# An adaptive-norm transformer block: gates and second shift and scale as rows from column-tiled products, first chunk modulated in SBUF, and a written-out sequence

## The chip, the cores and the metric

The kernel runs on one core of a Trainium2 chip. The metric is the device time of one execution in microseconds (us); a kernel's time is the median of its runs. Engines are named as in the profile: PE (TensorE, products), PEld (its weight loads), DVE (VectorE), ACT (ScalarE), POOL (GpSimd), SP (SyncE, which here issues nearly all DMAs).

## The reference

One sequence of 2048 rows of 640 values goes through windowed attention and a gated MLP. A vector c gives shifts, scales and gates for both. All inputs are bfloat16.

```
mod = silu(c) @ w_mod                      # 640 -> 6 x 640
sa, ca, ga, sb, cb, gb = mod
h = layernorm(x) * (1 + ca) + sa
x = x + ga * (attention(h @ wqkv) @ wo)    # 32 heads of 20, causal, window 256
h = layernorm(x) * (1 + cb) + sb
x = x + gb * ((sigmoid(h @ w_gate) * (h @ w_up)) @ w_down)   # hidden size 1536
```

## The kernel before

The rows are worked in 8 chunks of 256. For each chunk: normalize (DVE, line 811; POOL for some, 808), turn so that features lie on partitions, multiply by 1 + ca and add sa (chunks 0 and 1: turned by PE, and modulated by ACT or DVE on the way out of PSUM, lines 849 and 850; later chunks: turned by a transposing DMA, line 818, and modulated in SBUF, lines 826 and 827), project to q, k and v, attend, project with wo, add to x, normalize again, turn by DMA into h2T, modulate with shB and scB, and run the MLP. Scores use a 32-row tiling of PE and one PSUM tile S of four banks, which exp (ACT, line 1005) empties; products of probabilities and V (line 706, E and V) use a 32-column tiling. All other products take a PSUM bank of the pool M, of which there are four.

The gates are folded into weights: wo is scaled by ga (line 1228) and w_down by 0.5 gb (line 1163), both through one tile gbc, which holds the gate's 640 values on all 128 partitions.

How w_mod is used. It is loaded in four parts: part 0 (first shift and scale) into the place of w_down, part 1 (ga and sb) into that of w_up, part 2 (cb) into that of hh, part 3 (gb) into that of w_down again, once part 0 is used. silubc holds silu(c) repeated along a free axis. `mod_cols` makes a shift or a scale as a column, with w_mod as the stationary operand: five 128-column blocks by five slices, 64 equal result columns each, of which one is kept. `mod_bc` makes a gate on all partitions, with silubc (128 columns) as the stationary operand and w_mod as 320 moving columns: two halves by five slices, and two scalings into gbc (line 753). `mod_bc` and `mod_cols` run once for ga and sb, and once for gb and cb. The first shift and scale are made by similar products into S, copied to mA (line 776). Ahead of these, PE runs products on zeros that only keep it busy (lines 686 and 697).

What sets the order of the work. Every instruction group is recorded with its engines, its cost and its dependencies. `schedule` then places the groups one after the other by a table of priorities (PRIO), with a planner's model of costs, latencies and DMA bandwidth. Each engine runs its own list in order; waits between engines are semaphores. DMAs are placed in the lists of SP or ACT like instructions: a DMA that waits holds up what stands behind it on that engine. Tile slots are handed out by the planner too.

Of the kernel before, what the change touches and what calls it, by code (L numbers as in the profile page):

```python
# [51 lines left out]
class Tile:  # L52
    __slots__ = ("pool", "name", "res", "slot", "ops", "left", "rel", "prev", "mate")
# [27 lines left out]
class Prog:  # L81
# [8 lines left out]
    def op(self, eng, fn, dur, reads=(), writes=(), prio=50.0, lat=0.05, work=None, tmin=0.0, extra=(), tag="", hold=(),  # L90
# [13 lines left out]
        o.prio = PRIO[self.seq] if self.seq < len(PRIO) else prio  # L104
# [46 lines left out]
    def schedule(self):  # L151
# [3 lines left out]
        cand = {e: {} for e in ENGS}  # L155
# [6 lines left out]

        def arm(o):
            t = o.tmin
            for d in o.deps:
                t = max(t, d.end + (0.0 if (d.eng == "pe" and o.engs == ("pe",)) else d.lat))
            o.ready = t
            for e in o.engs:
                cand[e][o.seq] = o

        def slot_time(pool, s):
            ten = pool.tenant[s]
            if ten is None:
                if not all(x.done for x in pool.init[s]):
                    return None
                return max([x.end + x.lat for x in pool.init[s]], default=0.0)
            if ten.left:
                return None
            return max(x.end + x.lat for x in ten.rel)

        def slots_for(o):

            st = 0.0
            taken = {}
            got = []
            for t in o.tiles:
                if t.slot is None and t.mate is not None:
                    if any(g[0] is t for g in got):
                        continue
                    bs = None  # L190
                    for s in range(0, len(t.pool.tenant), 2):
                        ra, rb = slot_time(t.pool, s), slot_time(t.pool, s + 1)
                        if ra is not None and rb is not None and (bs is None or max(ra, rb) < bs[0]):
                            bs = (max(ra, rb), s)
                    if bs is None:
                        return None
                    got += [(t, bs[1]), (t.mate, bs[1] + 1)]
                    st = max(st, bs[0])
                elif t.slot is None:
                    bs = None  # L200
                    used = taken.setdefault(t.pool, set())
                    for s in range(len(t.pool.tenant)):
                        if s in used:
                            continue
                        rt = slot_time(t.pool, s)
                        if rt is not None and (bs is None or rt < bs[0]):
                            bs = (rt, s)
                    if bs is None:
                        return None
                    used.add(bs[1])  # L210
                    got.append((t, bs[1]))
                    st = max(st, bs[0])
                else:
                    for x in t.prev:
                        st = max(st, x.end + x.lat)
            return st, got

        for o in self.ops:
            if o.nleft == 0:
                arm(o)  # L220
        n = len(self.ops)
        placed = 0
        while placed < n:
            best = None
            for e in ENGS:
                c = cand[e]
                if not c:
                    continue
                lst = []
                tmin = None  # L230
                for o in c.values():
                    st = max(free[e] + (SWITCH if e == "pe" and o.mode != pemode else 0.0), o.ready)
                    if e == "dve" and o.port:
                        st = max(st, free["pool"])
                    elif e == "pool":
                        st = max(st, portend)
                    if o.isdma:
                        st = max(st, bw - QMAX)
                    if o.tiles:
                        got = slots_for(o)  # L240
                        if got is None:
                            continue
                        st = max(st, got[0])
                    lst.append((st, o))
                    if tmin is None or st < tmin:
                        tmin = st
                if not lst:
                    continue
                eps = PE_EPS if e == "pe" else 0.04
                pick = min((x for x in lst if x[0] <= tmin + eps), key=lambda x: (x[1].prio, x[1].seq))  # L250
                if best is None or pick[0] < best[0]:
                    best = (pick[0], e, pick[1])
            if best is None:
                left = [(o.tag, o.engs, [t.pool.name for t in o.tiles if t.slot is None]) for e in ENGS
                        for o in cand[e].values()][:40]
                raise RuntimeError(f"no op can be placed: {placed} of {n}: {left}")
            st, e, o = best
            for x in o.engs:
                cand[x].pop(o.seq, None)
            o.eng = e  # L260
            for t, s in slots_for(o)[1]:
                ten = t.pool.tenant[s]
                t.prev = list(t.pool.init[s]) if ten is None else list(ten.rel)
                t.slot = s
                t.pool.tenant[s] = t
# [7 lines left out]
            if o.isdma:  # L273
                turn = o.dlat > 3.0
                bw = max(st + o.dlat, bw + (MIXED if turn != lastturn and bw > st + o.dlat else 0.0)) + o.work
# [13 lines left out]
            placed += 1  # L289
# [12 lines left out]
            for x in o.succ:  # L302
                x.nleft -= 1
                if x.nleft == 0:
                    arm(x)
# [90 lines left out]
def c_pe(n):  # L396
# [3 lines left out]
PE_EPS = 0.14  # L400
PRIO = [
# [106 lines left out]
TR1 = 2  # L508
NPH = 2
NPQ = 2  # L510
PQ = ()
KEEP = 3
DSAFE = 1.0
MIXED = 0.39
NPB = 0
OUTE = ("sp", "act")
XE = ("sp", "act")
MW = 64
AFTER = 1
NOW = 1  # L520
# [10 lines left out]
def build(nc, A_x, A_wqkv, A_wo, B_x, B_w_gate, B_w_up, B_w_down, c, w_mod, out, S=2048):  # L531
# [298 lines left out]
    def pe_transposes(src, dst, sc, sh, Rmod, prio, a, ln="a"):  # L830
        last = []
        for dt in range(NDT):
# [10 lines left out]
            if a == 0 and dt == 3 and ln == "a":  # L843
                fills.append(fill(2 * FILL, [o]))
# [440 lines left out]
```

## Time and profile before

| what | value |
|---|---|
| median of 3 runs | 337.96 us |
| lowest and highest run | 336.16 and 338.79 us |
| the profiled execution: span | 333.9 us |
| median less that span | 4.1 us |
| PE, DVE, ACT, POOL busy | 325.6, 222.4, 229.3, 180.5 us |
| granted PE clock | full from 7 us to the end |
| bytes moved by DMA | 37.73 MB, of them 20.97 MB read from HBM |

The profile is one execution. Its span runs from the first to the last instruction; a run's time holds some us more, and the profiled execution's own time outside of its span is not listed, so it is compared by its span. A busy PE need not be at its peak, since products overlap: the distance from start to start of consecutive products says what one costs. Idle time counts only on the engine that sets the end.

The DMA engines are 70% to 90% busy in the first 80 us, in which all weights are loaded, and 0% to 50% later:

```profile
DMA  7999998984653773047125501501320303102101
```

### The profile page before, as it was taken

Reading aid. Unit: us, or ns where it says so; the run is one execution under the profiler, and the core shown is the slowest. Engines: PE = TensorE matmul, PEld = TensorE weight load, DVE = VectorE, ACT = ScalarE, POOL = GpSimd, SP = SyncE. Lnnn points to the kernel's source line nnn. Section 1 sums busy time; section 2 is a strip of 40 time slices with the busy share of each in tenths; the row PEclk is TensorE's granted clock in tenths of the full one; section 3 lists DMA queues with packets and bytes.
Section 4 is the critical chain, followed back from the end, with each engine's and each line's share of the span. In section 5 each row is a group of like instructions: output and inputs, shape, how many; then the busy total and the mean of one; then the engine's idle time right before and its main releaser. Section 6 shows DMA issues by size and latency. Waiting matters only on the chain.

```text
span 333.9 us, 10066 instructions
## 1 busy us (share of the span) xinstructions
PE 325.6 (98%) x4142; PEld 232.0 (69%) x4142; DVE 222.4 (67%) x445; ACT 229.3 (69%) x218; POOL 180.5 (54%) x259
## 2 busy tenths in 40 slices
PE   7899989998999999999999999999999999999996
PEld 2667646665786667766776776776776777887885
DVE  5389987999969845874486638465856295746323
ACT  1597977878768787888689967895695869221220
POOL 5038988996468764656565656665454667001000
PEclk9999999999999999999999999999999999999999
DMA  7999998984653773047125501501320303102101
GB/s 239 380 375 313 239 261 178 289 187 74 120 97 80 120 124 89 23 101 101 66 61 105 100 26 42 117 22 43 71 67 22 104 2 77 42 24 61 41 0 39
DMA packets 72694, 37.73 MB, mean 113 GB/s; under 512 B 46538, under 2 KB 71370, under 8 KB 72650
## 3 DMA queue, kind: packets, MB, share of 16 engines
q1 hardware_dynamic: 71056, 35.31, 43.9%
q10 hardware_dynamic: 1594, 1.80, 1.7%
q8 instruction: 32, 0.52, 0.6%
q14 instruction: 12, 0.10, 0.1%
HBM read 20.97 MB, written 5.24 MB: 79 GB/s over the span
## 4 chain that ended last, share of the span: by engine, by line
PE 86%; DVE 6%; DMA 3%; issue 2%; SPq 1%; ACT 0%; DVEq 0%
PE M L705 70%; PE S L706 8%; PE M L706 6%; DMA wd<-in_w_mod_dram 3%; PE S L686 2%; SPq L603 1%; DVE st L791 1%; DMA x<-in_A_x_dram 1%; DVE Tn L1059 1%; DVE T L1052 1%; DVE On L1061 1%; DVE x L811 1%; PE S L705 1%; DVE stg L885 1%; DVE h2T L827 0%
## 5 line engine op out<-in xcount | busy, mean ns | idle before, releaser
L1005 ACT ACTIVATE E<-S 128x2048 bf16<-128x2048 f32 x90 | 169.1, 1878 | 44.5 <-PE S L706 42.7
L1013 POOL TENSOR_SCALAR_AFFINE_SELECT E<-E 128x512 bf16<-128x512 bf16 (+2 forms) x90 | 78.2, 869 | 40.2 <-ACT E L1005 40.1
L1015 POOL TENSOR_SCALAR_AFFINE_SELECT E<-E 128x512 bf16<-128x512 bf16 (+1 forms) x84 | 68.5, 815 | 47.7 <-ACT E L1005 44.4
L705 PE MATMUL M<-h2T,wg 128*128 128x256 bf16 x480 | 64.8, 273 | 1.0 <-DVE h2T L827 1.0
L705 PE MATMUL M<-h2T,wu 128*128 128x256 bf16 x480 | 65.2, 273 | 0.0
L1182 DVE SCALAR_TENSOR_TENSOR hh<-sig,M 128x512 bf16<-128x512 f32 x48 | 32.6, 681 | 44.4 <-ACT sig L1180 24.4
L705 PE MATMUL M<-wd,hh 128*128 128x320 bf16 (+2 forms) x396 | 58.4, 295 | 0.0
L705 PEld LDWEIGHTS M<-h2T,wg 128*128 128x128 bf16 x480 | 45.0, 98 | 10.6 <-issue 2.3
L705 PEld LDWEIGHTS M<-h2T,wu 128*128 128x128 bf16 x480 | 45.3, 98 | 9.4 <-issue 3.0
L1180 ACT ACTIVATE sig<-M 128x512 f32<-128x512 f32 x48 | 28.3, 596 | 29.0 <-PE M L705 29.0
L705 PEld LDWEIGHTS M<-wd,hh 128*128 128x128 bf16 x396 | 37.1, 98 | 14.5 <-issue 1.5
L706 PE MATMUL S<-QT,KT 20*128 20x256 bf16 (+1 forms) x960 | 35.9, 245 | 0.2
L1201 DVE TENSOR_TENSOR x<-M,x 128x320 bf16<-128x320 f32 (+2 forms) x33 | 15.7, 479 | 23.4 <-PE M L705 22.9
L791 DVE BATCH_NORM_STATS2 st<-x 128x6 f32<-128x320 bf16 x64 | 28.3, 475 | 3.6 <-DMA x<-in_A_x_dram 3.5
L1052 DVE STREAM_TRANSPOSE T<-M 128x512 f32<-128x512 f32 x32 | 21.3, 697 | 12.7 <-PE S L706 12.0
L706 PEld LDWEIGHTS S<-QT,KT 20*128 20x128 bf16 x960 | 14.1, 92 | 20.1 <-ACT E L1005 12.1
L705 PE MATMUL M<-wk,hT 128*128 128x320 bf16 x160 | 26.6, 300 | 0.1
L705 PE MATMUL M<-wq,hT 128*128 128x320 bf16 x160 | 25.7, 299 | 0.2 <-issue 0.2
L705 PE MATMUL M<-wv,hT 128*128 128x320 bf16 x160 | 25.3, 300 | 0.1
L705 PE MATMUL M<-wo,oT 128*128 128x320 bf16 x160 | 24.1, 300 | 0.0
L706 PEld LDWEIGHTS M<-E,V 128*32 128x32 bf16 x960 | 20.0, 97 | 4.2 <-issue 2.6
L706 PE MATMUL M<-E,V 128*32 128x256 bf16 (+1 forms) x960 | 22.8, 246 | 0.2 <-issue 0.2
(78 smaller groups left out, 316.5 us busy)
## 6 DMA issues: line engine op xcount, KB each, us to landing
x<-in_A_x_dram SPq DMA_DIRECT2D x20, 160.0 KB
doc<-On SPq DMA_DIRECT2D x64, 40.0 KB
wd<-in_w_mod_dram SPq DMA_DIRECT2D x6, 320.0 KB
wd<-in_B_w_down_dram SPq DMA_DIRECT2D x4, 480.0 KB
wu<-in_w_mod_dram SPq DMA_DIRECT2D x5, 320.0 KB
out_dram<-x SPq DMA_DIRECT2D x10, 160.0 KB
oT<-doc SPq DMA_DIRECT2D x8, 192.0 KB
wg<-in_B_w_gate_dram SPq DMA_DIRECT2D x2, 576.0 KB
```

What stands on the lines that cost most here:

```text
L603: return e.dma_start(dst(), src())
L686: ins = e.matmul(p_S.aps[0][:, 3, :], Eall[:, 0, 0:128], Eall[:, 0, 128:640], start=True, stop=True)
L705: return e.matmul(o, l, r, start=st, stop=sp, skip_group_check=True)
L706: return e.matmul(o, l, r, start=st, stop=sp, tile_position=tp, skip_group_check=True)
L791: A("dve", lambda e, g, bi=bi, j=j: e.bn_stats(v(bi * 12 + j * 6, 6), src[bi].ap[:, j * 320:(j + 1) * 320]), 0.48, reads=[src[bi].r()], wr ...
L1005: A("act", lambda e, eng: e.activation(E.ap[:], Sp.ap[:], ACT.Exp, scale=SM_SCALE), 1.876, reads=[Sp.r()], writes=[E.r()], prio=3, tag=f"e ...
L1013: return e.affine_select(ap, ap, pattern=[[0, ap.shape[1]], [1, 128]], compare_op=ALU.is_ge, fill=0.0, base=0, channel_multiplier=-1)
L1015: return e.affine_select(ap, ap, pattern=[[0, ap.shape[1]], [-1, 128]], compare_op=ALU.is_ge, fill=0.0, base=-1, channel_multiplier=1)
L1052: A("dve", lambda e, g, h=h: e.transpose(T1.ap[:, 512 * h:512 * h + 512], X[h].ap), 0.694, reads=[X[h].r()], writes=[T1.r(h)], prio=3.5, t ...
L1180: A("act", lambda e, g, pg=pg, sg=sg: e.activation(sg.ap[:], pg.ap[:], ACT.Tanh, scale=0.5), c_act(512), reads=[pg.r()], writes=[sg.r()], ...
L1182: A("dve", lambda e, g, pu=pu, sg=sg, f0=f0: e.scalar_tensor_tensor(out=hh.ap[:, f0:f0 + 2, :], in0=sg.ap[:].rearrange("p (a b) -> p a b", ...
L1201: A("dve", lambda e, g, ps=ps, bi=bi, c0=c0, n=n: e.tensor_tensor(x1[bi].ap[:, c0:c0 + n], ps.ap[:, 0:n], x1[bi].ap[:, c0:c0 + n], op=ALU. ...
```

## The change

1. Both gates, the second shift and the second scale come from one kind of product, `mod_tiles`. The stationary operand is 32 columns of silubc, in one of four column tiles; each tile takes 160 columns of w_mod, and the result is a row, 32 times over, in each of four groups of 32 partitions. One call makes a gate and a shift (or scale): 5 slices x 2 x 4 = 40 products, as one group that waits for all its slices.
2. A gate's row (`mod_gate`) is scaled into `grow`, stored to DRAM (1280 bytes) and loaded back to all partitions of gbc. A shift or scale (`mod_turn`) is turned to columns by DVE's 32x32 transpose, its blocks picked so that feature t*128+p comes to partition p.
3. silubc is 64 wide, not 128. 
4. Chunk 0: its turned x is copied out of PSUM without shift and scale, and modulated in SBUF by DVE, ACT or POOL.
5. The table of priorities goes; the place and engine of every group are written out (PLAN, one number for each: 5 times the group's number plus the engine's), and `schedule` only follows it. The order differs on all engines. Among other things c's load is the first DMA on ACT, ahead of x; on SP the first part of w_mod goes ahead of x; PE runs two products on zeros before it turns c, and twelve after it (before: eight, and six after); part 3 of w_mod is issued behind the first transpose of chunk 2; all five scalings of wo are on DVE (before: two, with three on POOL).
6. Some of the planner's costs differ (DMA work and latency); they have no effect but through PLAN's slots.

```diff
+    def mod_tiles(parts, prio):
+        ps = Tile(p_M, "modt")
+
+        def fn(e, g):
+            ins = None
+            for kt in range(NDT):
+                for n, (i, c0, turned_) in enumerate(parts):
+                    src = wm_ap[i][:, kt, c0:c0 + D]
+                    for j in range(4):
+                        if turned_:
+                            r = src.rearrange("p (t g c) -> p g t c", g=4, c=32)[:, j]
+                            o = ps.ap[32 * j:32 * j + 32, n * 160:n * 160 + 160].rearrange("p (t c) -> p t c", c=32)
+                        else:
+                            r = src[:, j * 160:j * 160 + 160]
+                            o = ps.ap[32 * j:32 * j + 32, n * 160:n * 160 + 160]
+                        ins = mm(e, o, silubc[:, kt, 0:32], r, kt == 0 and n == 0, kt == NDT - 1, tp=(0, 32 * j))
+            return ins
...
+    def mod_gate(ps, n, factor, prio):
+        g = dram(f"gate{prio}", [4, 160])
+        Rd = R("gdram")
+        A("dve", lambda e, _: e.tensor_scalar(grow[:], ps.ap[:, n * 160:n * 160 + 160], factor, None, op0=ALU.mult),
...
+        dma(lambda: g, lambda: grow[0:128:32, :], 0.05, reads=[R_grow], writes=[Rd], prio=1, tag="gout", dur=0.42)
+        dma(lambda: gbc[:], lambda: g.rearrange("(o a) b -> o (a b)", o=1).to_broadcast([128, D]), 0.45, reads=[Rd], writes=[R_gbc],
...
+    def mod_turn(dst, ps, n, prio, plus, Rdst):
+        A("dve", lambda e, _: e.transpose(mt[:], ps.ap[:, n * 160:n * 160 + 160]), c_dve(160), reads=[ps.r()], writes=[R_mt], prio=8,
...
+        A("dve", lambda e, _: e.tensor_scalar(dst[:], mt[:].rearrange("p (t c) -> p t c", c=32)[:, :, 0], plus, None, op0=ALU.add), 0.2,
...
     def pe_transposes(src, dst, sc, sh, Rmod, prio, a, ln="a"):
...
+            if a == 0:
+                evac(lambda dt=dt: dst.ap[:, dt, :], lambda ps=ps: ps.ap[:, 0:256], 256, [ps.r()], [dst.r(dt)], 1, f"{ln}hTe{a}")
+                continue
...
             turned[a] = pe_transposes(src, t, scA, shA, [R_mA], 1, a)
+            if a == 0:
+                modulate(t, scA, shA, [R_mA], 1, "a", a, src)
...
-    o1 = mod_bc(1, 0, 1.0, 18)
-    psB = Tile(p_M, "modB")
-    cB, o2 = mod_cols(1, 640, psB, 18)
...
+    psB, o1 = mod_tiles([(1, 0, False), (1, D, True)], 18)
+    mod_gate(psB, 0, 1.0, 18)
+    mod_turn(shB, psB, 1, 18, 0.0, R_shB)
...
-    o3 = mod_bc(3, 0, 0.5, 19)
-    psC = Tile(p_M, "modC")
-    cC, o4 = mod_cols(2, 0, psC, 19)
...
+    psC, o3 = mod_tiles([(3, 0, False), (2, 0, True)], 19)
+    p_hh.init[1].append(o3)
+    mod_gate(psC, 0, 0.5, 19)
+    mod_turn(scB, psC, 1, 19, 1.0, R_scB)
```

More of the change, by code (lines that the diff above doesn't have):

```diff
@@ L52 @@
 class Tile:
-    __slots__ = ("pool", "name", "res", "slot", "ops", "left", "rel", "prev", "mate")
+    __slots__ = ("pool", "name", "res", "slot", "ops", "left", "rel", "prev", "mate", "at")
     def __init__(self, pool, name):
@@ L178, in slot_time @@
                 return None
[L179 to L185, printed above, removed]
-            for t in o.tiles:
[L187 to L259, printed above, removed]
-            o.eng = e
[L261 to L265, printed above, removed]
@@ new lines, in schedule @@
+        assert sorted(x // 5 for x in PLAN) == list(range(len(self.ops)))
+        for code in PLAN:
+            o, e = self.ops[code // 5], ENGS[code % 5]
+            assert e in o.engs and all(d.done for d in o.deps), (o.tag, e)
+            st = max(free[e] + (SWITCH if e == "pe" and o.mode != pemode else 0.0), o.tmin)
+            for d in o.deps:
+                st = max(st, d.end + (0.0 if d.eng == "pe" and o.engs == ("pe",) else d.lat))
+            if e == "dve" and o.port:
+                st = max(st, free["pool"])
+            elif e == "pool":
+                st = max(st, portend)
+            if o.isdma:
+                st = max(st, bw - QMAX)
+            for t in o.tiles:
+                if t.slot is None:
+                    place(t)
+                    if t.mate is not None:
+                        st = max(st, t.mate.at)
+                st = max(st, t.at)
+            o.eng = e
```

105 lines of the change are left out of this document (45 added, 60 removed), and 215 rows, old and new, of tables (PLAN, PRIO).

## The prediction

> **What bounds the kernel now.** I read the busy shares first, then TensorE's waits, then the timeline of TensorE and the chain of waits. Busy shares and the whole list of TensorE's waits:
>
> ```profile
> PE 325.6 (98%) x4142; PEld 232.0 (69%) x4142; DVE 222.4 (67%) x445; ACT 229.3 (69%) x218; POOL 180.5 (54%) x259
> ```
> ```profile
> PE S L686 <- DVE E L681: 1.7, 1, 1.7
> PE M L705 <- DMA wd<-in_w_mod_dram: 1.3, 1, 1.3
> PE M L705 <- DVE h2T L827: 1.0, 2, 0.6
> PE M L705 <- DVE hT L850: 0.6, 1, 0.6
> PE M L705 <- DVE stg L885: 0.4, 1, 0.4
> PE M L705 <- issue: 0.2, 1, 0.2
> PE M L706 <- issue: 0.2, 1, 0.2
> ```
>
> TensorE is the bound: it waits 5.4 us in 333.9, and after 83 us never. So two things can move the end: products taken out of its stream, and the few waits before 83 us. These timeline rows (start, length, engine, line, what) price both:
>
> ```profile
> 10.75 0.38 PE L697 MATMUL S<-E 128*128 128x512 bf16 x1
> 11.76 0.28 PE L705 MATMUL M<-ident,x 128*128 128x128 bf16 x2 [0.63 <-DVE hT L850]
> 12.26 1.52 PE L705 MATMUL M<-wq,hT 128*128 128x320 bf16 x10 [0.21 <-issue]
> 13.61 0.84 PE L705 MATMUL M<-wk,hT 128*128 128x320 bf16 x5
> ...
> 28.54 0.89 PE L705 MATMUL M<-silubc,hh 128*128 128x64 bf16 x25
> 29.27 0.31 PE L705 MATMUL M<-silubc,wu 128*128 128x64 bf16 x5
> ```
> ```profile
> 45.34 0.43 PE L705 MATMUL M<-wq,hT 128*128 128x320 bf16 x2
> 47.06 1.12 PE L705 MATMUL M<-wd,silubc 128*128 128x320 bf16 x7 [1.29 <-DMA wd<-in_w_mod_dram]
> ...
> 55.48 1.50 PE L706 MATMUL M<-E,V 128*32 128x256 bf16 x64 [0.16 <-issue]
> 56.92 0.40 PE L706 MATMUL S<-QT,KT 20*128 20x256 bf16 x8
> 57.25 2.89 PE L705 MATMUL M<-wo,oT 128*128 128x320 bf16 x20
> ```
>
> Lengths overlap, so I count from start to start: a 320-column product costs (13.61-12.26)/10 = 0.135 us, a 64-column one (29.27-28.54)/25 = 0.029, and 64 column-tiled products of attention (half of 256, half of 128 columns) 1.44.
>
> **The change, part by part.**
>
> *Products out, products in.* Out go 20 products of 320 columns (two gates, two halves, five slices) and 50 of 64 (shift and scale): 20 x 0.135 + 50 x 0.029 = 4.15 us, all in TensorE's stream. In come 2 x 40 of 160 columns in 32-column tiles. The row at 55.48 is 16 groups of four neighbouring tiles, 8 of 256 and 8 of 128 columns: 3072 columns in 1.44 - 0.1 us for a change of tiling (8 score products take 0.33 at 56.92, where 2 x 0.107 would do) = 0.44 ns a column, so 160 columns are 0.070 a group. 20 groups are 1.4, and two changes of tiling some 0.2: 1.6. Net **-2.6**. If four tiles ran one after the other it would be 80 x 0.070 = 5.6, net +1.4; if the changes of tiling vanish, -2.75. I take -2.6, since the E,V row has the same tile shape. A page speaks against it: the Trainium skill, TensorEngine Tiling (Array Packing), Restrictions and Gotchas, says column tiling excludes the fast weight load. The trace does not bear a cost out: weight loads of E,V average 97 ns against 98 for full ones and lie beside the products.
>
> *The wait at 45.34.* The gate's w_mod slice is issued at 38.62, behind four stores of attention results that wait for VectorE until 33.06 and behind four loads of w_up, and lands 8.39 us later, which TensorE awaits for 1.29. The chain of waits:
>
> ```profile
> 31.83 1.23 DVE On L1061
> 33.06 0.39 DVE stg L885
> ...
> 38.62 8.39 DMA wd<-in_w_mod_dram
> ```
>
> In the changed order both of its DMAs stand on SP right behind the first transpose of chunk 2, ahead of gate store, results and all but one load of w_gate and w_up. That transpose waits for a normalize which follows the first gate block, about 26 us; 8.4 us later is about 35, and the second block is due near 40. Gone: **-1.3** (bounds -1.5 and 0). What is late next there is nothing I can name. The first block now needs all five slices of w_mod at its first product; the last lands at 22.8 in this trace, and the new queue has 0.4 us less ahead of it, the block being due at 23.5: no cost, at most 0.5.
>
> *The start.* Plain copies of the turned x no longer wait for shift and scale. Before, the copy of mA at 10.95 is followed by PSUM evacuations of 0.5 us each on two engines, and wq starts at 12.26. After, one modulation of 0.43 (VectorE), two of 0.60 (ScalarE) and one of 0.56 (GpSimd) follow, and the first four products need only one from each of VectorE and ScalarE: 10.95 + 0.2 + 0.6 + 0.1 = 11.85. VectorE has two copies of 0.4 ahead of mA, which come free as TensorE turns x: cover 10.1 to 10.9, tight. **-0.4**. The other end: c's column is wanted after two warm-up products, not eight; its DMA took 2.4 us from issue, so TensorE stands from 2.1 to about 3.2 while its clock is still low (0.427 us a 512-column product until 6.9, 0.216 from 7.1). If that puts off the full clock by 3 us, the twelve others and the shift products cost up to 1.0 more. Bounds -0.6 and +1.0; -0.4 because the clock came at 7.0 and the first weights at 8.3.
>
> *The first MLP.* TensorE waits 0.37 and 0.61 at 81.7 for modulated h2T. VectorE's chain to it held a wait for an x load (0.78 at 71.35). In the new order no such load stands ahead, TensorE has 17.7 us of products between the first output projection's end and that point, and the chain (residual adds and statistics 3, power after the masks 6, normalize 1, SP past four transposes of 1.25, DMA 2.6, modulation 1.5) comes to some 15 to 19. I take half: **-0.5** (0 and -1.0).
>
> *Scores.* Exp holds the one score buffer: scores never start closer than 2.40 us (17.67 to 20.07, 139.38 to 141.78). By products alone the new order would put them 1.84, 2.22, 2.26 apart at 28 to 37 us. Pushing each to 2.40 gives 1.5 us in all, the old order 1.2: **+0.3** (0 to +1.0).
>
> *The gate's way.* Per gate: one 160-column scaling (0.3, the 320-column row is 0.48), two small turns (0.3 and 0.2), a store and a broadcast load, in place of two rows of 0.48 and a copy of 0.1. All on VectorE beside products. The five scalings of wo go to VectorE (5 x 0.53, before 2 x 0.53 there and 3 x 1.42 on GpSimd): +1.6 there, hidden behind TensorE's 6 us of products before wo; uncovered at most +1.6. SP has the store behind a transpose at about 32, and the load at about 38, behind three result stores; behind the load stand w_up, transposes of chunk 3, the second result stores and oT. With 31 to 36 us full of bulk loads, the store lands at about 36, so SP does not wait for it, and the load at about 42.5. VectorE comes to the first scaling at about 44. **0**.
>
> Sum: -2.6 - 1.3 - 0.4 - 0.5 + 0.3 = -4.5, so the span is 329.4. The profiled execution spans 333.9 and the median of the runs is 337.96, 4.1 above; the end (last product, add, store) is unchanged, so I carry the 4.1 over: **333.5 us**.
>
> **Rivals.**
>
> *The gain is given back at the first MLP (337).* The removed products all lie before 50 us, and the first MLP hangs on VectorE, 90% busy from 58 to 92 us. If that chain, not TensorE, sets the point at 81.7, then a shorter stream only waits longer there. For it: the two waits at 81.7. Against: the output projection itself comes 3 us of products earlier, and the late x load is out of the chain. Only about 1 us would be left.
>
> *The gate comes late (339.5, slower).* VectorE stands in order at the scaling of wo until the broadcast has landed; behind it are evacuations of chunk 2's q and k, whose PSUM banks TensorE needs. It decides from a landing at 44 us on, at a microsecond each, and eats the whole gain from 48.5. Landings of 8.4 us from issue occur (above); with the store as slow, 32 + 8 + 8.4 = 48.4, and one more queue delay of 1.5 gives 50. Against: the bulk ahead of it is over by 41.
>
> *A late clock (334.6).* The start pays +0.7 in place of -0.4. The Trainium skill, TensorE: Matmul & The Clock Gate, Part 1, has a free-running window of 3.4 us that must be busy throughout; by it the broken warm-up would get its full clock between 6.6 and 10. The trace agrees in the size (1.72 to 7.0), and shows no broken warm-up.
>
> *Tiles do not overlap (337.5).* Net +1.4 in place of -2.6, the rest as above. Against: the row at 55.48.
>
> **How the numbers follow.** Forecast 333.5 with chance 0.58 (own range 331.3 to 334.7: bounds of waits and start), first MLP 0.17, late clock 0.13, late gate 0.07, no overlap 0.05. A measurement can tell about 1% (3.4 us). Faster by over 1% is below 334.6: most of the forecast, half of the late clock, 0.61. Slower is above 341.3: the far part of the late gate and several at once, 0.04. Same: 0.35. The range of 331.0 to 337.4 leaves out the late gate, part of the first MLP and of no overlap, and 0.04 below.
>
> **What would show it.** Two blocks of 40 products 32x160 of 0.7 to 0.9 us each; no wait for w_mod; wq starting at 11.7 to 12.0; full clock before 8; the first MLP below 77 with under 0.5 us of waits; the wo scaling without a DMA wait; score starts never under 2.4 apart. Wrong it would be by a VectorE wait for gbc, by a block of 2.8 us, or by waits at the first MLP of over 2 us.

## The result, and the profile after

The changed kernel takes 338.56 us (median of 20 runs, 336.69 to 340.99); the kernel before took 336.73 beside it (20 runs, 335.88 to 338.85). The ratio is 1.0045 with a 95% interval of 1.0023 to 1.0067: slower by half a per cent, and 5 us above the forecast. The profiled execution spans 335.2 us (before: 333.9) and lies 2.1 us below its own time of 337.29, so it is one of the faster of the 20.

First TensorE's busy share and the DMA row of the page of after, then the list of what TensorE waited for (total, times, longest):

```profile
PE 322.9 (96%) x4152; PEld 230.2 (69%) x4152; DVE 219.9 (66%) x438; ACT 230.3 (69%) x221; POOL 180.7 (54%) x268
...
DMA  7999999999560348116334410624022304122101
```
```profile
PE M L653 <- DMA oT<-doc: 1.8, 1, 1.8
PE M L653 <- DVE T L1015: 1.5, 2, 1.2
PE S L634 <- DVE E L629: 1.3, 1, 1.3
PE M L653 <- DVE stg L848: 1.2, 1, 1.2
PE M L653 <- DVE x L1164: 1.1, 1, 1.1
PE M L653 <- issue: 1.1, 1, 1.1
...
```

TensorE is 2.7 us less busy, as the removed products ask. The wait for w_mod is gone, and so are the two for h2T. In their place stand five that before did not have, or only at 0.4 and less: for the attention result oT, for a PSUM bank that a transposed read frees (T), for q and k to be turned (stg), for a residual add (x), and inside the start ("issue", of which more below).

To see when the time comes back I add up, for both traces, what TensorE's products would take back to back (start-to-start distances of 0.135 us for 320 columns, 0.109 for 256, 0.056 for 128, 0.029 for 64, a quarter of that for tiled ones, 0.1 for a change of tiling), and subtract that sum from the actual start of each product. The difference is TensorE's lag in us:

| point in the sum of products | 30 | 42 | 50 | 56 | 65 | 75 | 85 | 120 | 200 | 315 |
|---|---|---|---|---|---|---|---|---|---|---|
| before | 1.30 | 1.94 | 3.86 | 4.14 | 4.14 | 4.85 | 6.28 | 6.59 | 7.63 | 8.40 |
| after | 1.77 | 3.70 | 4.07 | 5.91 | 6.63 | 8.23 | 8.21 | 10.29 | 11.41 | 12.25 |
| all repairs together (an experiment) | 0.82 | 3.53 | 3.50 | 3.62 | 4.72 | 5.54 | 5.50 | 6.86 | 7.99 | 8.85 |

The sum itself falls from 322.42 to 319.86, by 2.56 us. The lag at the end rises by 3.85. Together +1.3, which is the difference of the spans. After 120 the lags run alike, so all that matters happens earlier. The timeline of TensorE shows what was gained and the first and third loss:

```profile
11.28 0.70 PE L653 MATMUL M<-wq,hT 128*128 128x320 bf16 x4 [0.37 <-POOL hT L784]
13.05 1.11 PE L653 MATMUL M<-wq,hT 128*128 128x320 bf16 x7 [1.07 <-issue]
...
24.30 0.88 PE L654 MATMUL M<-wu,silubc 128*32 128x160 bf16 x40
25.10 1.12 PE L653 MATMUL M<-wq,hT 128*128 128x320 bf16 x7
...
56.53 1.66 PE L653 MATMUL M<-wo,oT 128*128 128x320 bf16 x11 [1.79 <-DMA oT<-doc]
```

A block of 40 column-tiled products takes 25.10 - 24.30 = 0.80 us. The first four products of wq start at 11.28, 1.0 earlier than before, but the fifth only at 13.05. What TensorE waits for, there and later, is in the timelines of VectorE and of GpSimd:

```profile
11.14 1.81 DVE L784 TENSOR_SCALAR hT<-hT,mA 128x256 bf16<-128x256 bf16 x1
...
34.48 1.57 DVE L712 TENSOR_SCALAR shB<-mt 128x5 f32<-128x5 f32 x1
...
45.78 1.40 DVE L1189 TENSOR_TENSOR wo<-wo,gbc 128x640 bf16<-128x640 bf16 x2
...
76.30 2.38 DVE L1126 TENSOR_TENSOR wd<-wd,gbc 128x640 bf16<-128x640 bf16 x3
...
108.96 1.86 DVE L768 TENSOR_SCALAR x<-x,st 128x640 bf16<-128x640 bf16 x2 [0.80 <-POOL st L755]
```
```profile
11.93 0.94 POOL L574 MEMSET Tn<- 128x1024 bf16 x1
...
33.80 2.22 POOL L976 TENSOR_SCALAR_AFFINE_SELECT E<-E 128x2048 bf16<-128x2048 bf16 x1 [1.14 <-ACT E L968]
```

The same modulation takes 0.35 at 10.42; here it takes 1.81 and ends at 12.95, just behind GpSimd's row of memsets, which begins at 11.06 and ends at 12.87. The last step of the turn, 128x5 elements, takes 1.57 and ends at 36.05, as GpSimd's mask does (33.80 + 2.22 = 36.02); its twin for scB takes 0.37 elsewhere. Before, these values came out of PSUM, in 0.10 and 0.16. A read from PSUM beside the same mask was not held: the evacuation of stg at 34.08 took 0.48. Behind the step of the turn stand a transpose and the evacuation of q and k that TensorE awaits at 37.62 for 1.22. Third: in the chain of waits (start, length, what) stands a transfer,

```profile
52.71 3.68 DMA oT<-doc
```

oT was issued at 51.47 before and landed 2.37 later; after, it stands on SP behind a load of w_down, an x load and a transpose of 1.77 us, is issued at 52.71 and needs 3.68. Ahead of these SP also stood 1.7 us at a store of results (last section). The rest of the loss is on VectorE, where order and GpSimd come together: at the first MLP three scalings of w_down (2.38 us) stand ahead of a transpose that frees a PSUM bank (TensorE waits 1.25 at 79.62, or 1.41 if counted from start to start), and at 109 two normalizations (1.86) ahead of two residual adds (1.14 at 111.28, or 1.30 from start to start). One such scaling takes 0.49 and one such normalization 0.43 where GpSimd is not at work beside it, so about 0.9 of the 2.38 and 1.0 of the 1.86 is time beside GpSimd's instructions. How much of these two waits is the order and how much GpSimd was not separated.

### The profile page after: what moved, and what is told of

Read it like the earlier page. It is cut to its first block, busy times and chain, and to the rows that moved or that the text cites. A ratio compares the mean times of both kernels' runs of the same rounds, so it can differ in the third digit from the quotient of the medians.

```text
span 335.2 us, 10090 instructions
## 1 busy us (share of the span) xinstructions
PE 322.9 (96%) x4152; PEld 230.2 (69%) x4152; DVE 219.9 (66%) x438; ACT 230.3 (69%) x221; POOL 180.7 (54%) x268
## 4 chain that ended last, share of the span: by engine, by line
PE 85%; DVE 7%; DMA 3%; issue 2%; ACT 1%; SPq 1%; POOL 0%; ACTq 0%; DVEq 0%
PE M L653 69%; PE S L654 8%; PE M L654 6%; PE S L634 1%; DMA h2T<-x 1%; ACT E L968 1%; DMA oT<-doc 1%; DVE st L748 1%; DVE wd L1126 1%; DVE On L1024 1%; DVE x L768 1%; DVE stg L848 1%; DMA c_row<-in_c_dram 1%; DVE hT L784 1%; DVE x L1098 0%
## 5 line engine op out<-in xcount | busy, mean ns | idle before, releaser
L976 POOL TENSOR_SCALAR_AFFINE_SELECT E<-E 128x512 bf16<-128x512 bf16 (+2 forms) x90 | 75.3, 846 | 39.1 <-ACT E L968 38.9
L978 POOL TENSOR_SCALAR_AFFINE_SELECT E<-E 128x512 bf16<-128x512 bf16 (+1 forms) x84 | 67.1, 810 | 45.0 <-ACT E L968 44.9
L653 PE MATMUL M<-h2T,wu 128*128 128x256 bf16 x480 | 71.2, 273 | 1.2 <-DVE T L1015 1.2
L653 PE MATMUL M<-h2T,wg 128*128 128x256 bf16 x480 | 69.4, 273 | 0.0
L653 PEld LDWEIGHTS M<-h2T,wu 128*128 128x128 bf16 x480 | 44.5, 98 | 12.5 <-issue 3.8
L653 PE MATMUL M<-wq,hT 128*128 128x320 bf16 x160 | 26.9, 299 | 2.6 <-DVE x L1164 1.1
L653 PE MATMUL M<-wk,hT 128*128 128x320 bf16 x160 | 27.9, 300 | 0.4 <-DVE st L750 0.4
L653 PE MATMUL M<-wv,hT 128*128 128x320 bf16 x160 | 27.1, 300 | 0.1
L653 PE MATMUL M<-wo,oT 128*128 128x320 bf16 x160 | 25.2, 300 | 1.8 <-DMA oT<-doc 1.8
L848 DVE CAST stg<-M 128x320 bf16<-128x320 f32 x38 | 17.6, 476 | 9.5 <-PE M L653 9.4
```

Source lines behind the costliest of these rows:

```text
L653: return e.matmul(o, l, r, start=st, stop=sp, skip_group_check=True)
L848: return e.tensor_copy(dst(), src())
L976: return e.affine_select(ap, ap, pattern=[[0, ap.shape[1]], [1, 128]], compare_op=ALU.is_ge, fill=0.0, base=0, channel_multiplier=-1)
L978: return e.affine_select(ap, ap, pattern=[[0, ap.shape[1]], [-1, 128]], compare_op=ALU.is_ge, fill=0.0, base=-1, channel_multiplier=1)
```

## The experiments

Orders are given as rows of an engine's list, in the form line, operation, out<-in. Ratios are to the kernel before, measured beside each kernel. Line numbers are each kernel's own and differ by up to five from the changed kernel's.

**The products alone, in the order of before.** The tiled blocks replace the old products where these stood; c, chunk 0, scores and transfers keep before's order, with the gate's store and load put in on SP:

```
+mod_tiles 0, mod_tiles 1
-mod_bc x4, mod_cols x10
 SP:
+gate<-grow
 hT<-x
+gbc<-gate
 hT<-x
```

> The kernel before, in its own sequence, with the column-tiled products alone: one block of 40 ahead of the first pv step, one ahead of a score set near 50 us, the gate by DRAM, the chunk-0 modulation on the way out of PSUM as before, the turned rows read by GpSimd, wo's scaling moved behind the gate's arrival. Theory 'sequence' (the products save 2.6 us of TensorE's stream, and the other parts of the change cost more than that in waits): the 2.6 us and the 1.3 us wait for w_mod show, 332.5 to 334.5 against 336.7. Rival 'absorbed' (chains of waits set the end, saved products are worth nothing): 336 to 337.5. Rival 'the trip costs' (the gate by DRAM delays what follows): above 337.5, with a DMA wait ahead of wo's scaling.

Measured: 343.03, ratio 1.0192 (1.0161 to 1.0223). The load waits for the store's landing (34.13): behind a transpose issued at 29.55, SP issues nothing until 34.15, and the stores of results and everything else wait: x8 lands at 50.1 in place of 47.4. VectorE evacuates late, and TensorE pays twice, 1.48 at 30.2 and 2.59 at 52.3, the second time with its clock as well. Timeline, and the same stretch by windows (bounds and length; busy and instructions of PE, PEld, DVE, ACT, POOL; granted clock; DMA share; GB/s):

```profile
52.25 0.71 PE L653 MATMUL M<-wk,hT 128*128 128x320 bf16 x2 [2.59 <-DVE stg L843]
```
```profile
52.00:54.00 2.00, 1.75 (x21) 0.82 (x22) 0.73 (x4) 0.44 (x1) 1.17 (x3) 0.50 0.80 154
54.00:56.00 2.00, 2.00 (x9) 1.16 (x8) 0.70 (x2) 1.44 (x1) 0.49 (x1) 0.50 0.72 160
```

The placement was at fault, so a second version has the load behind w_mod's last part, where SP comes to it after the store has landed:

```
 SP:
+gate<-grow
 hT<-x x2
 ...
 wd<-in_w_mod_dram 128x3x640
+gbc<-gate
 x<-in_A_x_dram x2
```

> As e1, in which SyncE stood 4.6 us at the load of the gate (its store had landed only 6 us after its issue) and the block stood where VectorE's statistics had to wait for it. Here the gate's load is issued just ahead of x8 near 39 us, the rows are read behind the statistics, and wo is scaled by VectorE in its idle time from 46 us on. Theory 'sequence': now the products show, 333 to 335.5 against 336.7, with no stall over 1.5 us near 30 and 52 us. Rival 'the trip costs': 338 or more, a DMA wait ahead of wo's scaling or of oT. Rival 'absorbed': 336 to 337.5.

Measured: 342.77, ratio 1.0166 (1.012 to 1.0211), with single executions from 338.28 (mean clock 1.00; this one is profiled) to 343.51 (0.99). The profiled one spans 336.5, still 2.6 above before, with a shorter stream: TensorE reaches what it waits for earlier and waits 0.6 to 1.6 more at six places, four times for VectorE (24.9, 29.2, 49.9, 78.9) and twice for ScalarE (26.5, 46.9). Both versions are far above what was expected of them, and in neither did the products' gain show. Where another engine ends the wait that follows, products taken from ahead of it only lengthen that wait. The profiled execution is the fastest of its six; what the four near 343 lost besides is not seen.

**More products in the stream.** Each block gets 64 tiled products more, into columns of the result bank that nobody reads:

```
+for k in range(64):
+    j = k % 4
+    ins = mm(e, ps.ap[32 * j:32 * j + 32, 320:480], silubc[:, 0, 0:32], wm_ap[parts[0][0]][:, 0, 0:160], ...)
```

> The changed kernel with 64 more products of 32x160 in each of the two blocks, into unused columns of the same bank (the output is untouched): 20 ns each by the trace, 1.3 us a block, what the old products cost beyond the new ones. Theory 'sequence' (TensorE's stream sets the end, a saving there counts in full): 338.6 + 2.6 = 341.2. Rival 'absorbed': 338.6 to 339.2.

Measured: 342.52, ratio 1.0199 (1.0164 to 1.0234), 4 to 5 us over the changed kernel. The first block's length grows from 0.88 to 1.98, which is 16 groups of 0.070: the four tiles run side by side, also at this length. The other part is new waits that no engine ends:

```profile
31.16 0.57 PE L654 MATMUL M<-wk,hT 128*128 128x320 bf16 x3 [1.24 <-issue]
...
47.94 1.01 PE L655 MATMUL M<-wd,silubc 128*32 128x160 bf16 x47 [1.70 <-issue]
```

2 x 1.10 + 1.24 + 1.70 = 5.1, which is also the difference of the two profiled spans (340.3 and 335.2), though single waits shifted beside it (oT's from 1.8 to 0.4). So time added to TensorE's stream does count to the end in this kernel. That a saving counts too is another matter, which only the version with all repairs below shows. With 104 tiny products in a row TensorE was short of instructions in the middle of the second block (47.94) and 4 us behind the first (31.16); that its fetch is what failed is argued, not shown.

**Chunk 0 as before.** Modulation on the way out of PSUM again, the rest as changed:

```
-            if a == 0:
-                evac(lambda dt=dt: dst.ap[:, dt, :], ...)
-                continue
...
-            if a == 0:
-                modulate(t, scA, shA, [R_mA], 1, "a", a, src)
```

> The changed kernel with chunk 0 modulated on the way out of PSUM, as before the change, all else in the changed order. Theory 'VectorE waits for GpSimd': a read of PSUM is not held up by GpSimd's memsets (11.06 to 12.87 us), so the split start of 11.28 and 13.05 us becomes one start near 11.9 us, 1 us less: 337.6. Rival 'modulation in SBUF is a gain of 0.4 us, as predicted': 339.

Measured: 338.36, ratio 1.0041 (1.0015 to 1.0067). wq starts once, at 12.64, not near 11.9 as expected. This does not settle what modulating in SBUF is worth, since the edit moved the hold to another place: with no modulation on GpSimd its memsets ran at once, from 7.43 to 9.75, and VectorE's normalization of x beside them took 2.40 (7.52 to 9.92) in place of 0.43, for which TensorE waited 0.91 at 10.33.

**VectorE out of GpSimd's way.** GpSimd's memsets go ahead of its first statistics (it idles there), and the last step of both turns goes to GpSimd:

```
-        A("dve", lambda e, _: e.tensor_scalar(dst[:], mt[:], ...
+        A("pool", lambda e, _: e.tensor_scalar(dst[:], mt[:], ...
 POOL:
+stg<- x1, V<- x8, Tn<-
 st<-st 128x2
 ...
-stg<- x1, V<- x8, Tn<-
```

> The changed kernel with only the two places where VectorE's new work on SBUF operands stands behind GpSimd: the memsets of the start moved ahead of the first statistics, and the last step of shift and scale given to GpSimd. Theory 'VectorE waits for GpSimd' (1.23 us at the start, 1.39 us at 37.6 us): the second modulation takes 0.35 instead of 1.81 us, and 336 to 337 is left of 338.6. Rival 'order of the DMAs alone' (the waits at 56, 80 and 111 us made the loss): the two waits go and come back later, 338 to 338.6.

Measured: 336.66, ratio 1.0006 (0.998 to 1.0031). The modulation takes 0.35 in place of 1.81, and shB on GpSimd 0.25; both waits are gone. But the next limit stands 1.5 us behind where the second of them was. Timelines of TensorE and of VectorE:

```profile
39.18 0.84 PE L654 MATMUL M<-E,V 128*32 128x256 bf16 x32 [1.29 <-DVE KT L848]
```
```profile
37.62 0.35 DVE L784 TENSOR_SCALAR hT<-hT,mA 128x256 bf16<-128x256 bf16 x1 [1.52 <-DMA hT<-x]
```

VectorE now waits for the second transposing load of chunk 2 (in the changed kernel issued at 31.5, landed at 37.77; before 31.93 and 35.3), with KT's evacuation behind it.

**Three places of order.** oT's loads ahead of the bulk load of w_down; the transpose that frees T ahead of the scalings of w_down; the residual adds at 109 ahead of the normalizations:

```
 SP:
-wd<-in_B_w_down_dram 128x3x640
 x<-in_A_x_dram, QT<-stg, oT<-doc x2
+wd<-in_B_w_down_dram 128x3x640
 DVE:
 h2T<-h2T,scB,shB
+T<-M 128x512 x2
+h2T<-h2T,scB,shB
 wd<-wd,gbc 128x640 x3
-h2T<-h2T,scB,shB
-T<-M 128x512 x2
...
-x<-M,x 128x320
-x<-x,st 128x640 x2
-x<-M,x 128x320 x2
+x<-M,x 128x320 x3
+x<-x,st 128x640 x2
```

> The changed kernel with three places of its order mended and nothing else: w_down's first load behind oT's two loads on SyncE, VectorE's transposes of the second pv step ahead of three scalings of w_down at the first MLP (wait of 1.41 us at 79.6 us), two residual sums ahead of two normalizations (1.30 us at 111.3 us). Theory 'order': the two VectorE waits go and do not come back within 5 us, oT lands 1 us earlier: 338.6 - 2.7 - 1 = 335. Rival 'absorbed': another wait of the same size follows each, 338 to 338.6.

Measured: 337.69, ratio 1.0019 (0.9993 to 1.0045). The wait for oT is gone and that at 111 us halved (1.30 to 0.66, from start to start); the MLP's moved to a v product that awaits an evacuation by ScalarE (1.06 at 79.61) and to a score (0.74). The result lies nearer the rival's 338 than the expected 335, and its interval touches the changed kernel's.

**Transposes of chunk 2 first, then bulk.** On SP both transposes go ahead of w_mod's part 3 and the loads of w_up, with GpSimd's memsets and the turns' last step as two experiments above:

```
 SP:
-hT<-x
+hT<-x x2
 wd<-in_w_mod_dram 128x3x640, wd<-in_w_mod_dram 128x2x640
+gate<-grow
+hh<-in_w_mod_dram
 wu<-in_B_w_up_dram
-hh<-in_w_mod_dram
-hT<-x
-gate<-grow
```

> e10 with the second transposing load of chunk 2 issued ahead of w_mod's last part, wm2's last part and w_up's first part on SyncE. In e10 the wait of 1.4 us behind the shift's last step was followed by one of 1.32 us at 39.2 us, where VectorE stood at the head of its queue for hT of chunk 2 (landed 37.6 us, 6.1 us after its issue). Theory 'sequence' (the early w_mod load that took the old wait away is paid for by that transpose): hT of chunk 2 lands near 35.5 us, the 1.32 us goes, w_mod's last part still lands ahead of its products at 42 us, 335.3 of 336.7. Rival 'DMA engines full': hT lands as late as before and the wait stays, 336.7.

Measured: 339.41, ratio 1.0077 (1.0046 to 1.0107). TensorE now has no stall from 29.6 to 49.3, and then the gate stops everything. Timelines of VectorE and TensorE, and windows:

```profile
47.07 1.78 DVE L1189 TENSOR_TENSOR wo<-wo,gbc 128x640 bf16<-128x640 bf16 x2 [4.04 <-DMA gbc<-gate]
```
```profile
49.31 0.45 PE L653 MATMUL M<-wq,hT 128*128 128x320 bf16 x2 [3.94 <-DVE stg L848]
```
```profile
50.00:52.00 2.00, 2.00 (x10) 1.16 (x8) 1.55 (x5) 0.00 (x0) 0.00 (x0) 0.50 0.87 282
```

The load of the gate was issued at 39.87 and landed at 46.97: 7.1 us for 1280 bytes spread to 128 partitions. VectorE was ready at 43.0. In the changed kernel VectorE is ready at 45.78, and the load landed at 45.69: the late gate is real and was covered by 0.1 us.

**The gate early.** Its store goes ahead of chunk 2's first transpose, its load right behind the second, on top of the last experiment (first), as the only edit of the changed kernel (second), and, on top of the first, with w_down behind oT and the order at 109 (third):

```
 SP:
+gate<-grow
 hT<-x x2
+gbc<-gate
 ...
-gate<-grow
...
-gbc<-gate
```

> e11 with the gate's two transfers moved forward on SyncE: the store right behind the row's copy (near 26 us, where SyncE stands idle), the load right behind the second transposing load of chunk 2. In e11 VectorE stood 4.04 us for the gate at 43.0 us (load issued 39.87, landed 46.97) and TensorE 4.02 us behind it. Theory 'the gate's way' (it was covered in the changed kernel only because VectorE arrived 2.6 us late itself): the gate lands before 40 us, the 4 us wait goes, 335 to 336 where e11 had 339.4. Rival 'DMA engines full' (whatever goes first, the last of the transfers needed by 50 us is late): another DMA wait of 2 us or more between 40 and 52 us, 338 or more.

> The changed kernel with nothing but the gate's two transfers moved forward on SyncE, as in e14. In the trace after the gate landed 0.09 us before the first scaling of wo began; if it lands later than that in other executions, those wait for it. Theory 'the gate's way decides here already': 337 or less where the changed kernel has 338.6, and a narrower spread. Rival 'not yet the last to arrive': 338 to 339, since VectorE is 2.6 us late for two other reasons.

> e14 with w_down's first load behind oT's loads and the two residual sums ahead of the two normalizations near 110 us. In e8 the wait of 1.89 us for oT went, and the wait of 1.30 us near 111 us became one of 0.66 us. Theory 'sequence': 1.5 to 2.5 us below e14, 333 to 334, faster than the kernel before. Rival 'absorbed': within 0.7 us of e14.

Measured: 338.9 (1.0052; 1.0018 to 1.0086), 338.1 (1.0024; 0.9986 to 1.0062) and 338.47 (1.0032; 0.9997 to 1.0067), the changed kernel beside them 338.23 (1.0044; 1.001 to 1.0078). None comes near what was expected of it (335 to 336, 337 or less, 333 to 334). In the first the gate lands at 37.24, and the next wait takes its place:

```profile
PE M L653 <- DMA oT<-doc: 4.0, 1, 4.0
```

> The changed kernel itself, on the chip of e14 to e16, so that they can be compared with it: 338.6, ratio 1.0045.

The changed kernel ran again as it is; its ratio repeats.

**The bulk loads behind oT.** One load of w_up and that of w_down go behind oT's, on top of the early gate with the transposes first (first), as the only edit (second), and on top of the first with the order at 109 (third); in the fourth a transpose of q and k goes behind oT too:

```
 SP:
-wu<-in_B_w_up_dram 128x3x768
 ...
-wd<-in_B_w_down_dram 128x3x640
 ...
 oT<-doc x2
+wu<-in_B_w_up_dram 128x3x768
 wu<-in_B_w_up_dram 128x2x768
+wd<-in_B_w_down_dram 128x3x640
```

> e14 with the second load of w_up's first part and the first of w_down behind oT's two loads on SyncE. In e14, e15 and the changed kernel SyncE stood 1.7 to 2.1 us at the fourth store of pv's second result until that w_up load had landed, and oT took 3.7 to 4.0 us to land against 2.37 in the kernel before. Theory 'oT's landing sets the end of the stretch up to 57 us': oT lands at 53.5 to 54.5 us instead of 57.3, the 4.10 us wait of TensorE shrinks by as much, 335 to 336 where e14 had 338.9. Rival 'another follows': oT lands earlier and the time stays within 1 us of e14's.

> The changed kernel with nothing but these two bulk loads behind oT's loads. Theory 'oT's landing': its wait of 1.2 to 1.9 us at 56 us goes, the waits of VectorE before it stay: 336.3 to 337 where the changed kernel has 338.2 to 338.6. Rival 'another follows': 338.

> e17 with the two residual sums ahead of the two normalizations near 110 us, which took a wait of 1.3 us down to one of 0.66 us in e8. Theory 'sequence': 0.6 below e17. Rival 'another follows': as e17.

> e19 with oT's two loads also ahead of one transposing load of chunk 2's q on SyncE, whose issue takes 1.5 us. In e5 that order made TensorE wait 2.54 us at 61.5 us for the stage buffer which that transpose frees, but there it was issued behind w_down's load as well. Theory 'oT's landing': oT a further 1.5 us earlier, and no wait over 1 us near 61 us, 0.5 to 1 below e19. Rival 'the transpose is the next to be late': the wait near 61 us is back with 1.5 us or more, e19's time or above.

Measured: 339.63 (1.0097; 1.0062 to 1.0131), 339.41 (1.0080; 1.0054 to 1.0106), 339.7 (1.0080; 1.0052 to 1.0109) and 339.15 (1.0076; 1.005 to 1.0102). None of the gains expected came. oT lands early enough (55.0 in the first, wait 0.4), but now the transposes of chunk 2's q and k have the bulk around them. They land at 62.9, where before had them at 57.3:

```profile
63.00 0.84 PE L653 MATMUL M<-wq,hT 128*128 128x320 bf16 x5 [2.85 <-DMA QT<-stg]
```

In the fourth this wait is 4.1 and the granted clock is 0.50 from 62 to 69 us.

**All repairs together.** GpSimd's memsets early, the turns' last step on GpSimd, oT's loads ahead of a transpose of q and k and of w_down, and the two orders on VectorE; the transposes, the gate and w_up stay where the change put them:

```
 SP:
-wd<-in_B_w_down_dram 128x3x640
 x<-in_A_x_dram
-QT<-stg
 oT<-doc x2
+QT<-stg
+wd<-in_B_w_down_dram 128x3x640
```

> The changed kernel with five places of its sequence mended: GpSimd's memsets of the start ahead of the first statistics, the last step of shift and scale on GpSimd, oT's loads ahead of w_down's first load and a transpose on SP, the transposes of the second pv step ahead of the scaling of w_down at the first MLP, and the two residual sums ahead of the normalizations near 109 us. The five waits stand at 1.2 + 1.4 + 1.9 + 1.4 + 1.3 = 7.2 us in the trace after. Theory 'sequence': most of it comes off, 332 to 335. Rival 'absorbed': each wait's end is followed by another, 337 to 338.6.

> The same kernel as e5 (335.41, ratio 0.9984). Theory 'sequence': again 335 to 336, below the changed kernel by 2.5 to 3 us; the typical execution's lag behind a stream without stalls is about 9.5 to 10.5 us at the end, against 12.3 to 14.2 in the changed kernel. Rival 'a lucky set': 337 to 338.

Measured: 335.41, ratio 0.9984 (0.9958 to 1.0011), and the same kernel again on another chip 335.2, ratio 0.9964 (0.9935 to 0.9994). That interval and the changed kernel's (1.0023 to 1.0067) do not meet. It is about 3 us faster than the changed kernel, and in the second set faster than the one before as well. Of the first set the profile shows an execution of 337.87, of the second one of 334.13. The first has a wait that the other does not have; timeline of the first, list of waits of the second:

```profile
61.41 0.84 PE L653 MATMUL M<-wq,hT 128*128 128x320 bf16 x5 [2.33 <-DMA QT<-stg]
```
```profile
PE M L654 <- DVE KT L848: 1.9, 1, 1.9
PE S L634 <- DVE E L629: 1.3, 1, 1.3
PE S L654 <- ACT E L968: 0.8, 1, 0.8
...
```

So even here a transfer near 60 us comes in time in one execution and late in another; executions lie from 333.34 to 339.1. The two part on SP: in the second a load of w_up landed at 46.10 and SP's fourth store of results did not stand, in the first it landed at 47.48 and the store was issued at 47.78. The second keeps the gain: the table above has its lag at 8.85, near before's 8.40, with a stream 2.56 shorter. This is what shows that the saving counts. The first, among the longest of its set (334.66 to 339.1), ends at a lag of 13.11. The repairs bring the ordinary execution down, which the medians and the ratios show, not each one.

**The last try** puts all bulk loads of 42 to 60 us behind the transposes of chunk 2's q and k and behind hT of chunk 4:

```
 SP:
-wu<-in_B_w_up_dram 128x3x768, wd<-in_B_w_down_dram 128x3x640, wu<-in_B_w_up_dram 128x2x768
 ...
 hT<-x 128x5x128
+wu<-in_B_w_up_dram 128x3x768, wu<-in_B_w_up_dram 128x2x768, wd<-in_B_w_down_dram 128x3x640
```

> e5 with the second load of w_up's first part, the second of its second part's and the first of w_down behind the transposing loads of chunk 2's q and k and of chunk 4 on SyncE (issued near 63 instead of 40 to 54 us; they are needed from 79 us on). Theory 'bulk loads among the transfers that the next step needs': those transposes land before 60 us, no DMA wait of TensorE over 0.5 us up to 65 us, 333.5 to 334.5, faster than the kernel before. Rival 'the number of transfers': as e5 or, with w_up late at the first MLP, slower than it by 1 us or more.

Measured: 337.39, ratio 1.0018 (0.9997 to 1.0038). Chunk 2's q and k are in time, chunk 3's are late, by 3.9 at 70.2. The bulk has to go somewhere.

## Why the prediction was wrong

It forecast 333.5 with a range up to 337.4; the time was 338.56. The span was to fall by 4.5 and rose by 1.3, 5.8 in all, of which 0.7 came back in what lies around the span (3.4 by the median, not 4.1). The median of before was 337.96 in the three runs that the forecast started from and 336.73 in twenty, so by the change alone the miss is larger: -4.5 forecast, +1.8 measured. By its own steps:

- *Products, -2.6*: right. The stream is 2.56 shorter, a block is 0.80 us, tiles overlap; the extra products show that the stream counts, and the version with all repairs that the saving can be kept.
- *The wait for w_mod, -1.3*: gone, as forecast. But the forecast wrote "What is late next there is nothing I can name". Late next were oT at 56.5 (1.8), then in several versions with oT in time the transposes of q and k at 61 to 63 (2.3 to 4.1), then in the last try those of chunk 3 at 70.
- *The start, -0.4*: +0.5 (lag at 30: 1.77 against 1.30). The first four products came at 11.28, earlier than the 11.85 worked out. The step put one VectorE modulation at 0.43, the mean of ten in the trace of before; alone it takes 0.35, and beside GpSimd's memsets it took 1.81. The sign was there: the same form on h2T averages 0.57 over twenty in that trace, with 0.35 as its median and 1.16 as its longest. A mean far above the median asks what held the long ones. The late clock did not come: from 7.36 on 64-column products run 0.029 apart, which is the full pace.
- *The gate's way, 0*: the failed step. Its terms were instruction counts by duration, "All on VectorE beside products". The gate itself cost nothing, by 0.1 us, where the forecast had a margin of 1.5 (landing at 42.5, scaling at 44). The turn beside it cost 1.4: 0.2 forecast for its last step, 1.57 taken while GpSimd held it, ahead of an evacuation that TensorE awaits. And moving SP's rows was costed at nothing for oT, which the same paragraph lists behind the gate's load; oT came 1.8 late.
- *First MLP, -0.5*: about -1.0 + 1.4 = +0.4. The h2T waits went, but the moved scalings stood ahead of T, with about 0.9 us of their time beside GpSimd.
- *Scores, +0.3*: 0.2 at most. TensorE waits once for the score buffer, 0.19 at 50.43.
- *Not in the sum at all*: 1.3 at 111 us, from residual adds moved behind normalizations, with about 1.0 us of their time beside GpSimd. The forecast looked at no order past 92 us.

In the forecast's terms the waits shrink by 1.3 + 0.4 + 0.5 and grow by 0.3, -1.9 in all; TensorE's lag grew by 3.85. The difference of 5.75 is the whole error of the span. None of the three signs that it named of being wrong appeared: no wait for gbc, blocks of 0.80 to 0.88, 1.25 at the first MLP. Nearest in size is the rival "the gate comes late" (339.5), but by luck: the gate cost nothing in this kernel, though the transposes-first version shows the mechanism at full size (4.04 us). "The gain is given back at the first MLP" (337) has the right kind of mechanism, with one place where the trace has five. "Tiles do not overlap" (337.5) is near in size too, and the tiles do.

How much of the loss each cause holds: the GpSimd repair takes 0.39% off the ratio (1.0045 to 1.0006), the order repair 0.26%, both together 0.6 to 0.8%. So the two add up to what both do together, though the intervals of the single steps touch the changed kernel's. They do not add up to the whole miss: the forecast asked for 333.5 in 337.96, a ratio of 0.987, and the repaired kernel is at 0.996 to 0.998. In the second profile of all repairs the lag is 8.85 where the forecast asked for some 6.5 (8.40 less 1.9), and its longest wait is 1.9 for an evacuation of KT; no version brought this rest back. Open remains whether the late transfers between 47 and 70 us are held by the engines' rate, which the DMA row has at 0.9 and more from 8 to 84 us (before: 0.8 and more up to 75; later both rows still reach 0.7 and 0.8 in single slices, more than the 50% of the part ahead), or by the order in which the queue serves them; no version separated the two.

## What to carry to other kernels

Where an engine is 98% busy, price a reorder by walking every queue past each thing that lands late, not by what the moved instructions cost: here the repaired waits at 37, 47, 56 and 63 us were each followed by another of 1.3 to 4 us, in the end for a transfer each time. A step moved from PSUM to SBUF on VectorE must be looked up against what GpSimd does at that moment. And a shorter stream pays only if the product after the removed ones has its operand.

## What the runs showed of the hardware

VectorE held by GpSimd: operations with all operands in SBUF ended with GpSimd's work, 0.03 to 0.18 us behind it, at 1.81 us in place of 0.35, 1.57 in place of 0.37 and, with chunk 0 as before, 2.40 in place of 0.43. The first was short again (0.35) once GpSimd's memsets were elsewhere; the second was moved to GpSimd itself (0.25). The Trainium skill, SBUF — State Buffer, Who interferes with whom, says that VectorE in its two-port mode and GpSimd share a port pair, that whoever issues first has it for the whole instruction, and that the other fully blocks. The trace agrees that it blocks; but VectorE was not let in between ten consecutive memsets of GpSimd (11.06 to 12.87), of which the first takes 0.41. At 76 to 78 us it did come in between GpSimd's instructions: the first two of the three scalings took 1.00 and 0.92, and each ended 0.34 behind one of GpSimd's.

The clock after a wait: TensorE's granted clock fell to 0.50 behind waits of 2.59, 2.84, 3.85, 3.94, 4.01 and 4.13 us in six of the experiments, and not behind 2.85 in another (clock 1.00 from 63 to 67 us) nor behind 2.33. Inside the kernel the stretches at 0.50 last 3.41 or 6.83 us and begin on a grid of 3.41 us that starts with the first record of full clock in each trace. On this grid the mixed outcome near 2.85 comes out: that wait lay across two windows (TensorE busy for 0.50 of the one from 58.43 to 61.84), and the wait of 2.84 lay in one (busy for 0.33 of 60.55 to 63.97). By the profile, each window at full clock with TensorE busy for up to 0.47 of it was followed by half the clock, and none with 0.48 or more was. One fall came without a long wait: with the transposes first, at 80.71, behind waits of 0.47 and 1.36 in one window that was busy for 0.46. The Trainium skill, TensorE: Matmul & The Clock Gate, Part 1, has a free-running window of about 3.4 us and half the clock after an idle one. The traces agree in the length and in that the window runs on its own; they differ in that it need not be idle, only busy for less than about half. A wait over 3.8 lost the clock each time.

Issues that stand: SP's fourth store of results was issued at 48.71, just behind the landing of a w_up load at 48.36 that had been issued at 40.58; in five other runs the same two stand 0.3 us apart (48.52 and 48.83, 49.17 and 49.46, 49.58 and 49.87, 48.34 and 48.65, 47.48 and 47.78). The second run with all repairs, where the load landed at 46.10, has no such stand. What ties them is not shown.
